# A fused routed-attention and SoLU kernel on one core: a new written order for all engines, and the first one-hot marks copied by three engines

## The chip, the cores and the metric

The kernel runs on one core of a Trainium2 chip. The metric is the device time of one execution in microseconds (us); lower is better. Before the change the median of three runs is 225.78 us (225.64 to 225.80).

The core has a matrix engine (PE, with its weight loads shown apart as PEld), a vector engine (DVE), a scalar engine (ACT), a general engine (POOL) and a queue that issues DMAs (SP). Each works through its own list of instructions in order and waits for the others by semaphores.

## What is computed

Attention with routing: queries and keys of each head are assigned to the nearest of 16 centroids, and a query attends only to keys of its own cluster. The result, read as 3072 tokens of 512 numbers, goes through a feed-forward layer with a SoLU activation and a layer norm.

```python
def _attn_ref(q, k, v, centroids):            # (4, 8, 768, 64), centroids (8, 16, 64)
    ...
    q_assign = np.argmax(np.einsum('bhsd,hcd->bhsc', q_n, c_n), axis=-1)
    k_assign = np.argmax(np.einsum('bhsd,hcd->bhsc', k_n, c_n), axis=-1)
    mask = q_assign[:, :, :, None] == k_assign[:, :, None, :]
    scores = scale * np.matmul(q, k.transpose(0, 1, 3, 2))
    scores = np.where(mask, scores, -1000000000.0)
    ...
    return np.matmul(attn, v)
def _moe_ref(x, w_in, w_out, g_ln):           # (3072, 512), (512, 1024), (1024, 512)
    h = x @ w_in
    ...
    solu = h * sm                             # sm is the softmax of h
    ...
    ln = (solu - mu) / np.sqrt(var + 1e-06) * g_ln
    return ln @ w_out
```

## The kernel before

Work is cut into pairs of heads, four pairs in each of four batches, written `b.p`. For a pair, queries (`i` = 0) and keys (`i` = 1) are loaded, turned so that the head dimension lies on the partitions, and cast to bf16 into a tile `qk`. Beside the 64 numbers of a head, `qk` holds one-hot marks of the token's cluster; the keys' marks and the queries' marks raise the score of matching clusters, so that one matmul gives scores that are already masked, and the exponential with a constant bias does the rest.

All work is described as small named operations. `Weave.add` records each with its engine, its cost in a planner and what it needs; `Weave.queues` puts them on the engines' lists in the order that the text `ORDER` gives: for each engine a row of kinds with repeat counts (`E12` is the next twelve operations of kind `E`). `AWAY` names the operations that run on another engine than their default. The planner's costs do not enter the order of one engine's list, which is read from the text. The kinds that matter here, with the function and line that issues them:

- `ld`, `lv`: loads of queries, keys, values on SP (L366 to 399, L527).
- `tp` (`turn_tokens`, L386, PE): the first batch's tokens turned by matmuls with the identity, into three banks of PSUM in turn; `xa` (`keep_tokens`, L393, ACT or DVE): the copy out of PSUM. The very first pair, `0.0`, is done in two halves, whose number is the last of the name. Later batches are turned by DVE: `xt` (L407).
- `ca` (`cast`, L431 ACT, L433 and L435 DVE or POOL): the cast into `qk`. A half has 64x384 elements, a whole one 64x768. `cv` (L532): the cast of the values. `bl` (L523), `z`, `zo`: memsets.
- `cl` (`clusters`, L450, L445, PE): the products with the centroids. Then a chain on DVE: `tb` turns them back (L459), `mx` takes the largest (L472), `oh` marks it (L484), `ot` turns the marks (L494). `pl` (`place`, L498 to 519) copies the marks into `qk`: four copies for each pair or half (L514; L506 for the other pairs of the first batch), on DVE, POOL, or as a DMA on SP. `place` knows DVE, POOL and SP before.
- `S` (`scores`, L601, PE) for a bank of 512 or 384 scores, `E` (`expo`, L607, ACT), `V` (`values`, L624, PE), `N` (`normalise`, L636 and L649, DVE). There are three score banks and nine tiles of exponentials, used in turn, so `S` waits for the `E` three before it, and `E` for the `V` that has read the tile nine before.
- The feed-forward layer works on blocks of 128 tokens, `f` from 0 to 23: `tx` turns the block (SP; for the last one PE, `ptx`, L688, and a copy on DVE, `tx23`, L691), `h` multiplies with `w_in` (L710, PE), `hm` takes the row maximum (L716, DVE), `ex` the exponential (L722, ACT), `u` the product (L727, DVE), `tu` turns it (SP; for the last two `ptu` on PE, L698, and copies `tu`, L704 DVE or L706 ACT), `bn` and `ag` are row statistics (L738 and L742, DVE), `at` and `al` the factor of the norm (POOL, L748 to 757), `y` multiplies with `w_out` (L771, PE), `sc` scales (L786 ACT or L788 DVE) and `ou` stores. `h` for the second half of block f waits for `u` of block f-1, since the two share a bank.
- `wm` and `fl` (L816) are matmuls on idle data at the start; `lo`, `li`, `wi`, `su`, `me`, `ce`, `gt`, `gk` prepare the weights of the layer.

Resolved into names, the order before begins and ends so:

```
PE    wm tp0.0.0.0 tp0.0.1.0 cp tp0.0.0.1 cl0.0.0 tp0.0.1.1 fl0..fl4 cl0.0.1 fl5..fl8 S0.0 ...
ACT   xa0.0.0.0 xa0.0.1.0 ca0.0.0.0.0 ca0.0.0.1.1 xa0.0.1.1 ca0.0.1.0.1 ca0.0.1.1.0 E0.0 ...
      E0.5 E1.3 E1.4 E1.5 xa0.2.1.0 xa0.2.1.1 E2.0 ...
DVE   cn cb xa0.0.0.1 ca0.0.1.0.0 tb0.0.0 mx0.0.0 oh0.0.0 ot0.0.0 pl0.0.0.1.1 pl0.0.0.0.0 tb0.0.1 ...
POOL  z1 ca0.0.0.0.1 ca0.0.0.1.0 pl0.0.0.1.0 pl0.0.0.0.1 cv0.0.1 z2 bl0.0.0 ...
DVE at the end
      ... hm21 sc17 u21 N38 ag19 ag20 bn21.0 tx23 hm22 bn21.1 sc19 u22 bn22.0 ag21 hm23 bn22.1
      tu22.0 ag22 u23 bn23.0 bn23.1 tu23.1 ag23 sc23.1
```

Of the kernel before, what the change touches and what calls it, by code (L numbers as in the profile page):

```python
# [22 lines left out]
class Weave:  # L23
# [18 lines left out]
    """
    ORDER["PE"] = """
        wm tp2 cp tp cl tp fl5 cl fl4 S3 tp2 S2 tp S cq S tp S2 tp2 S2 V3 S cl S tp2 V3 S gt S tp S
        tp S2 cl S2 V2 S V S2 tp S2 tp S2 V2 S V S2 cl S2 V2 S V2 S3 V S2 V2 S2 V S cl S3 su S2 V3 S
        V S3 V3 S2 V S su S2 V S V3 S3 me S3 V4 S3 cl S3 V4 S2 h S h S2 h S h S2 V3 S2 V h S h V S V
        S h S V S V S h S2 V3 S2 V h S2 h V2 S y3 S2 h3 S3 y V3 h V S2 V2 S cl S3 h2 S2 V3 S y2 S V
        h2 S V y2 S h S V h S2 h S y3 S2 y V3 h S3 cl V2 S V S y S2 y2 S3 V3 S y S2 V3 S2 cl S V S2
        V2 S h S2 V2 S V S h S2 V2 cl V2 S3 y2 S V S2 V y S2 y V2 S3 h2 S V h S h S2 V h S V S V y2
        S h V y2 S2 V S h3 S cl V S2 V2 S h V cl S3 h2 V y V S3 y2 V S h V3 S y S h S2 h2 S3 V2 y h  # L50
        S V S2 y V3 y S3 h3 y S3 V3 S h S V S V cl S V S h S cl V2 S3 y V2 S y S2 y V2 S3 h y V S3 V
        h V2 S3 cl S2 V2 S y3 S2 y S V3 S V S y S2 V S V3 S2 y2 S3 y V2 S2 h V2 S3 h3 S V S2 V y S V
        h2 V2 S y S2 y V y S h2 S3 cl h V S2 V3 S h V2 S3 h2 S y S2 V h S2 V y2 V4 S3 y h S2 h V h V
# [115 lines left out]
def kernel(  # L169
# [11 lines left out]
    nc = tc.nc  # L181
# [4 lines left out]
    NB = 32  # L186
# [1063 lines left out]
```

## Time and profile before

| | |
|---|---|
| median of the runs | 225.78 us |
| the profiled execution: time, span | 225.95 us, 223.9 us |
| busy: PE, DVE, ACT, POOL | 215.1, 197.3, 191.5, 127.1 us |
| granted PE clock | 1.00 throughout |
| first scores begin (L601, PE) | 10.16 us |
| last exponentials of scores begin (L607, ACT) | 200.6 us |
| last store issued | 221.3 us |

The span is the time from the first to the last instruction or transfer of the profiled execution; the rest of its time lies around it. Busy times are sums over one engine, which overlap with those of the others. The chain of waits follows the last instruction back to what released it, step by step.

### The profile page before, as it was taken

How to read it: one execution, taken by the hardware profiler on the slowest of the kernel's cores; microseconds unless marked ns; L12 is line 12 of the kernel's file. 1: busy time of each engine (PE TensorE's matmuls, PEld its weight loads, DVE VectorE, ACT ScalarE, POOL GpSimd, SP SyncE). 2: the span in 40 equal slices, each digit the busy share in tenths (PEclk: the TensorE clock that was granted, in tenths of full speed). 3: DMA queues.
4: the chain of work that ended last, by engine and by line, in shares of the span. 5: the costliest groups of instructions: out<-in, count | busy, mean ns of one | idle time of the engine just before them, and what ended most of it. 6: DMA issues, size and time to landing. Idle time of an engine off the chain costs nothing.

```text
span 223.9 us, 6574 instructions
## 1 busy us (share of the span) xinstructions
PE 215.1 (96%) x2388; PEld 148.1 (66%) x2420; DVE 197.3 (88%) x359; ACT 191.5 (86%) x371; POOL 127.1 (57%) x247
## 2 busy tenths in 40 slices
PE   7899999999999999999999999999999999999993
PEld 3576756677667678776677667777677687754442
DVE  3799899899999989999998989887998889888981
ACT  3689999999998999998889899999999998982362
POOL 3489843964794999547668634943895413031331
PEclk9999999999999999999999999999999999999999
DMA  7998989999898989999999999199931433766622
GB/s 152 353 318 147 249 199 275 290 243 158 132 199 140 232 130 165 193 189 177 183 218 168 184 195 195 65 174 232 236 64 28 79 70 120 96 146 170 176 97 94
DMA packets 125679, 38.80 MB, mean 173 GB/s; under 512 B 115016, under 2 KB 121168, under 8 KB 125648
## 3 DMA queue, kind: packets, MB, share of 16 engines
q1 hardware_dynamic: 123904, 37.87, 80.6%
q10 hardware_dynamic: 1744, 0.52, 1.0%
q8 instruction: 19, 0.31, 0.6%
q14 instruction: 12, 0.10, 0.2%
HBM read 23.11 MB, written 6.29 MB: 131 GB/s over the span
## 4 chain that ended last, share of the span: by engine, by line
PE 86%; ACT 5%; DVE 3%; issue 3%; DMA 1%; POOL 1%; ACTq 0%; DVEq 0%; POOLq 0%
PE sps L601 28%; PE hreg L710 18%; PE yps L771 16%; PE ops L624 14%; ACT e L607 5%; PE csc L450 4%; PE hreg L386 2%; PE hreg L574 1%; PE hreg L771 1%; DMA c_all<-in_centroids_dram 1%; PE csc L445 1%; DVE bs L738 1%; DVE u L727 1%; ACT xt L393 0%; PE hreg L584 0%
## 5 line engine op out<-in xcount | busy, mean ns | idle before, releaser
L607 ACT ACTIVATE e<-sps 128x512 bf16<-128x512 f32 (+1 forms) x294 | 151.0, 599 | 12.2 <-PE sps L601 10.2
L601 PE MATMUL sps<-qk 80*128 80x256 bf16 (+5 forms) x636 | 93.8, 264 | 1.8 <-POOL qk L514 0.7
L601 PEld LDWEIGHTS <-qk 80*128 80x128 bf16 (+1 forms) x636 | 60.2, 121 | 27.9 <-issue 9.0
L624 PEld LDWEIGHTS <-e 128*128 128x128 bf16 x1152 | 50.4, 97 | 12.3 <-issue 1.9
L624 PE MATMUL ops<-v,e 128*128 128x65 bf16 x1152 | 55.0, 193 | 0.1
L710 PE MATMUL hreg<-w_in_sb,xT 128*128 128x512 bf16 x173 | 49.1, 379 | 1.1
L771 PE MATMUL yps<-w_out_c,uT 128*128 128x512 bf16 x171 | 46.4, 379 | 0.6
L727 DVE TENSOR_TENSOR u<-e_sb,hreg 128x1024 bf16<-128x1024 bf16 x24 | 29.0, 1210 | 4.9 <-ACT e_sb L722 4.7
L514 POOL COPY qk<-oht 32x384 f32<-32x384 f32 (+1 forms) x50 | 24.4, 488 | 15.8 <-DVE oht L494 13.6
L738 DVE BATCH_NORM_STATS2 bs<-u 128x6 f32<-128x512 bf16 x48 | 31.5, 676 | 0.2
L716 DVE TENSOR_REDUCE nmax<-hreg 128x1 f32<-128x1024 f32 x24 | 29.0, 1209 | 2.6 <-PE hreg L710 2.2
L722 ACT ACTIVATE e_sb<-hreg,nmax 128x1024 bf16<-128x1024 f32 x24 | 26.9, 1120 | 4.5 <-DVE nmax L716 4.4
L433 POOL CAST qk<-xt 64x768 bf16<-64x768 f32 (+1 forms) x31 | 26.1, 842 | 5.5 <-DVE xt L393 3.9
L771 PEld LDWEIGHTS <-uT 128*128 128x128 bf16 x200 | 18.2, 97 | 12.3 <-DVE uT L704 0.7
L754 POOL TENSOR_SCALAR esq<-es,mv 128x1 f32<-128x1 f32 x24 | 8.5, 355 | 29.0 <-DVE mv L742 20.8
L435 POOL TENSOR_SCALAR qk<-xt 64x768 bf16<-64x768 f32 (+1 forms) x28 | 23.0, 820 | 1.7
L710 PEld LDWEIGHTS <-xT 128*128 128x128 bf16 x192 | 16.8, 97 | 9.4 <-issue 0.6
L407 DVE STREAM_TRANSPOSE xt<-raw 128x768 f32<-128x768 f32 x24 | 22.6, 953 | 0.2 <-DMA raw<-in_q_dram 0.2
L748 POOL TENSOR_SCALAR es<-esum 128x1 f32<-128x1 f32 x24 | 5.3, 221 | 27.6 <-ACT e_sb L722 27.1
L649 DVE TENSOR_TENSOR x<-ops,den 128x256 bf16<-128x256 f32 (+1 forms) x39 | 18.9, 486 | 1.3
L757 POOL TENSOR_TENSOR alpha<-esq,halves 128x1 f32<-128x1 f32 x24 | 13.5, 561 | 2.0
L786 ACT ACTIVATE y<-yps,alpha 128x512 f32<-128x512 f32 x13 | 9.0, 692 | 6.4 <-PE yps L771 6.0
(80 smaller groups left out, 170.1 us busy)
## 6 DMA issues: line engine op xcount, KB each, us to landing
vf<-in_v_dram SPq DMA_DIRECT2D x16, 384.0 KB, 4.4
out_dram<-y SPq DMA_DIRECT2D x23, 256.0 KB, 2.7
raw<-in_q_dram SPq DMA_DIRECT2D x50, 96.0 KB, 3.7
raw<-in_k_dram SPq DMA_DIRECT2D x50, 96.0 KB, 3.0
w_g<-in_moe_w_out_dram SPq DMA_DIRECT2D x4, 512.0 KB, 5.3
w_st<-in_moe_w_in_dram SPq DMA_DIRECT2D x4, 512.0 KB, 5.9
raw<-in_q_dram SPq DMA_DIRECT2D x3, 384.0 KB, 6.3
raw<-in_k_dram SPq DMA_DIRECT2D x3, 384.0 KB, 6.8
```

The costliest lines, as they stand in the source:

```text
L433: VEC[e].tensor_copy(dst, src)
L435: VEC[e].tensor_scalar(dst, src, scalar1=inv_C, scalar2=1.0, op0=Alu.mult, op1=Alu.mult)
L514: ins = VEC[e].tensor_copy(dst.bitcast(F32), src.bitcast(F32).unsqueeze(1) .to_broadcast([NB, 2, n // 2]))
L601: nc.tensor.matmul(sps_[n, k][:, c0:c0 + w], side(b, h // 2, 1, h % 2, keys)[r], side(b, h // 2, 0, h % 2, slice(s0 * P, s0 * P + w))[r])
L607: nc.scalar.activation(es[n, k][:, :w], sps_[n, k][:, :w], Act.Exp, scale=exp_scale, bias=-exp_scale)
L624: nc.tensor.matmul(opss[g][:, s, :VW], es[n, k][:, c0:c0 + P], v1[slot(b, h // 2)][:, h % 2, kt, :VW], start=(kt == 0), stop=(kt == n_t - 1))
L710: uses(nc.tensor.matmul(hreg[:, at(f, f2)[1], :], xTs[f][:, dc, :], w_in_sb[:, dc, f2 * FF2:(f2 + 1) * FF2], start=(dc == 0), stop=(dc == ...
L716: uses(nc.vector.tensor_reduce(ff[f, "nmax"][:], pair_of(f), axis=AXY, op=Alu.max, negate=True), *both(f))
L722: uses(nc.scalar.activation(ff[f, "e"][:], pair_of(f), Act.Exp, bias=ff[f, "nmax"][:], accum_out=ff[f, "esum"][:]), *both(f))
L727: uses(nc.vector.tensor_tensor(ff[f, "u"][:], ff[f, "e"][:], pair_of(f), op=Alu.mult), *both(f))
L738: nc.vector.bn_stats(ff[f, "bs"][:, f2, :], ff[f, "u"][:, f2, :])
L771: ins = nc.tensor.matmul(dst, ff[f, "uT"][:, at(f, f2)[0] * (n_fc // 2) + c, :], w_out_c[:, fc, cols], start=(fc == 0), stop=(fc == n_fc - 1))
```

## The change

The change writes a new `ORDER` for all five engines and a new `AWAY`, gives `place` a branch for ACT, and alters three of the planner's costs (which, as said, don't enter the lists).

```diff
     ORDER["PE"] = """
-        wm tp2 cp tp cl tp fl5 cl fl4 S3 tp2 S2 tp S cq S tp S2 tp2 S2 V3 S cl S tp2 V3 S gt S tp S
+        wm tp2 cp tp cl tp fl5 cl fl3 S3 tp2 S2 cq S tp S tp S2 tp S tp S V3 S cl tp2 V3 S gt S2 tp
...
     ORDER["DVE"] = """
-        cn cb xa ca tb mx oh ot pl2 tb mx oh ot xa3 bl cf cv xa zo xa2 tb ca mx oh gk N ot tb pl mx
+        cn cb ca2 tb mx oh ot pl2 tb mx oh ot xa2 ca xa cf xa2 ca tb mx xa gk oh ot N tb xa mx oh
...
-        hm sc u N ag2 bn tx hm bn sc u bn ag hm bn tu ag u bn2 tu ag sc
+        bn2 hm ag bn ag sc u N bn2 tx hm sc u bn2 hm ag tu ag tu u bn2 tu ag sc2
     ORDER["ACT"] = """
-        wa xa2 ca2 xa ca2 E12 xa2 E6 xa E58 ex E12 ex E8 ex E8 ex E3 sc E5 ca E2 ex E25 ex E9 sc E6
+        wa xa ca xa3 ca pl ca E9 xa E3 ca xa E6 xa E58 ex E13 ex E7 ex E10 ex sc E5 sc E6 ex E9 sc
...
     AWAY.update(dict.fromkeys("""
-        ca0.0.0.0.0 ca0.0.0.1.1 ca1.3.1.1 sc23.0 tu22.1 xa0.0.1.0 xa0.2.1.0 xa0.2.1.1 xa0.3.0.0
+        ca0.0.0.0.0 ca0.2.0.0 ca2.2.1.0 ca2.2.1.1 ca3.0.1.1 pl0.0.0.0.1 sc23.0 xa0.0.0.1 xa0.0.1.0
+        xa0.2.0.1 xa0.2.1.0 xa0.3.0.0
     """.split(), "ACT"))
...
         elif e == "SP":
             ins = nc.sync.dma_start(out=dst, in_=src.unsqueeze(1).to_broadcast([NB, 2, n]))
+        elif e == "ACT":
+            ins = nc.scalar.copy(dst, src.unsqueeze(1).to_broadcast([NB, 2, n]))
...
-    add("wm", "PE", 3.55, -1000, lambda e: [idle(FF2) for _ in range(6)])
+    add("wm", "PE", 3.9, -1000, lambda e: [idle(FF2) for _ in range(6)])
...
-                add(f"tp{t}.{hf}", "PE", 0.7 - 0.2 * hf if halves_of(b, p) else 0.36, first - 15 + i + hf,
+                add(f"tp{t}.{hf}", "PE", (0.5 if i * hf else 0.7) if halves_of(b, p) else 0.36, first - 15 + i + hf,
...
-                costs = ({"DVE": 0.3, "POOL": 0.41} if half else
+                costs = ({"DVE": 0.3, "POOL": 0.41, "ACT": 0.42} if half else
```

The number of `fl` in the text sets how many are made: nine before, eight after. Sixty-three operations change their engine. ACT takes `xa0.0.0.1`, `xa0.2.0.1`, one mark copy (`pl0.0.0.0.1`), the casts `ca0.2.0.0`, `ca2.2.1.0`, `ca2.2.1.1`, `ca3.0.1.1` and the scalings `sc2`, `sc3`, `sc6`, `sc8`, `sc10`, `sc13`, and gives away `xa0.2.1.1`, `ca0.0.0.1.1`, `ca1.3.1.1`, `sc11`, `sc12`, `sc14`, `sc22` and `tu22.1`. POOL's list goes from 212 to 205 operations. Seven mark copies are DMAs on SP, `pl1.0.1.0` and `pl1.0.1.1` the first, in place of four.

The lists begin and end so after the change:

```
PE    wm tp0.0.0.0 tp0.0.1.0 cp tp0.0.0.1 cl0.0.0 tp0.0.1.1 fl0..fl4 cl0.0.1 fl5..fl7 S0.0 ...
ACT   xa0.0.0.0 ca0.0.0.0.0 xa0.0.1.0 xa0.0.0.1 xa0.0.1.1 ca0.0.1.0.1 pl0.0.0.0.1 ca0.0.1.1.0 E0.0 ...
      E0.5 xa0.2.0.1 E1.3 E1.4 E1.5 ca0.2.0.0 xa0.2.1.0 E2.0 ...
DVE   cn cb ca0.0.0.1.0 ca0.0.1.0.0 tb0.0.0 mx0.0.0 oh0.0.0 ot0.0.0 pl0.0.0.1.0 pl0.0.0.1.1 tb0.0.1 ...
POOL  zo ca0.0.0.0.1 cv0.0.0 ca0.0.0.1.1 pl0.0.0.0.0 z1 bl0.0.0 ...
DVE at the end
      ... hm21 ag19 bn20.1 ag20 sc17 u21 N38 bn21.0 bn21.1 tx23 hm22 sc19 u22 bn22.0 bn22.1 hm23 ag21
      tu22.0 ag22 tu22.1 u23 bn23.0 bn23.1 tu23.1 ag23 sc22 sc23.1
```

80 lines of the change are left out of this document (40 added, 40 removed).

## The prediction

> **What bounds the kernel now.** I read the page first (busy shares, chain of waits), then the busy time of each engine by stage, then the timeline of the first 24 us and of the last 18.
>
> ```profile
> PE 215.1 (96%) x2388; PEld 148.1 (66%) x2420; DVE 197.3 (88%) x359; ACT 191.5 (86%) x371; POOL 127.1 (57%) x247
> ...
> PE 86%; ACT 5%; DVE 3%; issue 3%; DMA 1%; POOL 1%; ACTq 0%; DVEq 0%; POOLq 0%
> ```
>
> PE is busy 96% of the span and carries 86% of the chain that ended last. The change takes no PE work away but one filler matmul (`fl8`, about 0.07 us, inside a wait). So the time can change in three places alone: the start, where PE waits; the stretches where another engine fills up and PE waits for it; and the end, where PE's work is no longer the chain.
>
> ```profile
> core 0: us, PE busy (x) PEld busy (x) DVE busy (x) ACT busy (x) POOL busy (x), PEclk, DMA share, GB/s
> ...
> 18.00:22.00 4.00, 3.87 (x43) 2.20 (x41) 3.68 (x10) 4.00 (x11) 3.79 (x6) 1.00 0.72 94
> ...
> 26.00:30.00 4.00, 3.89 (x66) 2.93 (x64) 3.34 (x7) 4.00 (x9) 3.46 (x6) 1.00 0.72 141
> ...
> 45.00:50.00 5.00, 4.94 (x69) 3.82 (x68) 4.82 (x9) 5.00 (x11) 3.31 (x6) 1.00 1.24 261
> 50.00:60.00 10.00, 9.56 (x115) 7.38 (x115) 9.48 (x18) 9.95 (x20) 5.10 (x11) 1.00 0.83 138
> ```
>
> Read the fourth busy column: up to 60 us ACT is as full as PE. In these four rows (23 us) ACT is busy 22.95 and PE 22.26, so PE loses 0.74 us, 3.2%. In the seven rows of 20 us from 60 to 200 PE is busy 138.51 of 140 (1.1% lost) and ACT 130.05 (93%).
>
> **The start.**
>
> ```profile
> 6.85 0.56 DVE L393 COPY xt<-hreg 128x384 f32<-128x384 f32 x1 [0.66 <-PE hreg L386]
> ...
> 7.59 0.37 DVE L459 STREAM_TRANSPOSE cst<-csc 128x192 f32<-128x192 f32 x1
> ...
> 8.83 0.38 DVE L494 STREAM_TRANSPOSE oht<-oh 128x192 bf16<-128x192 bf16 x1
> 9.25 0.58 DVE L514 COPY qk<-oht 32x192 f32<-32x192 f32 x2
> ...
> 9.35 0.76 POOL L514 COPY qk<-oht 32x192 f32<-32x192 f32 x2 [0.77 <-DVE oht L494]
> ...
> 10.16 0.65 PE L601 MATMUL sps<-qk 80*128 80x384 bf16 x3 [0.73 <-POOL qk L514]
> ```
>
> The first cluster products end at 7.27 (their row: 6.74 and 0.53), yet DVE turns them back at 7.59: it is busy with `xa0.0.0.1` and a cast. After the change `xa0.0.0.1` is on ACT and both casts of DVE use data that are ready by 6.5, so the turn waits for PE alone. The later products that end at 15.80 are taken up at 15.90, so I count 0.10 and get 7.37: 0.22 earlier. The chain behind it is unchanged (7.59 to 9.21), and `ot0.0.0` ends at 8.99. Does the new ACT order delay the products? `ca0.0.0.0.0` (0.52) now stands ahead of `xa0.0.1.0`, which ends near 6.45 in place of 6.16; PE is at its transposes until 6.74, so nothing. Past that, 0.3 us of cover is left.
>
> The four mark copies: before two on DVE and two on POOL, to 10.11. After: two on DVE (9.03 to 9.60), one on POOL, one on ACT. POOL has two half casts (0.53 each) and `cv0.0.0` (0.50) ahead, from 7.40 to 9.05, and its mark takes 0.36, to about 9.5. A mark copy on ACT is in no trace; the ACT copy of 384 elements takes 0.48 and the 64x384 cast 0.52, the shortest ACT row (one element) 0.19; I take 0.50, which also ends at 9.6. With a cast (0.52) behind it the exponentials can start at 10.1. So the first scores go from 10.16 to about 9.70: **-0.45** (bounds 0 and -0.55).
>
> The Trainium skill (SBUF — State Buffer, Who interferes with whom) says that GpSimd and a VectorE copy in a two-port mode exclude each other for a whole instruction. By that rule the POOL mark would come behind both DVE marks, near 9.95, and the first scores near 10.05, a gain of 0.1. The rows above disagree: POOL's first copy ran from 9.35 to 9.71 across two DVE copies and took 0.36, against 0.34 for the same copy at 11.89 beside a DVE copy out of PSUM.
>
> **ACT up to 60 us.** How much of the 0.45 lasts depends on ACT, full from 10.5 on.
>
> ```profile
> 14.80 1.25 ACT L607 ACTIVATE e<-sps 128x384 bf16<-128x384 f32 x3 [0.72 <-PE ops L624]
> 16.44 0.86 ACT L393 COPY xt<-hreg 128x384 f32<-128x384 f32 x2 [0.39 <-PE hreg L386]
> ```
>
> After the change ACT gets `ca0.2.0.0` (a 64x768 cast, 0.84 by its one ACT row) ahead of `E2.0`. `xa0.2.0.1` moves into the 0.72 gap (0.40 saved behind it), about 0.12 of the second gap is used, the rest waits for `S2.0`, now behind V1. `E2.0`: -0.45 + 0.84 - 0.40 - 0.12 = **-0.13** (bounds -0.45 and +0.4).
>
> From 22 to 45 us ACT has six gaps behind late PE (0.16, 0.16, 0.18, 0.38, 0.14, 0.16: 1.18). PE is late there mostly behind DVE and POOL: `cl0.3` waits 0.42 for `xa0.3.1.1`, `V6.0` 0.41 for N2, `V10.0` 0.62 for N4, and `S4.0` 0.61 for the POOL mark that ends at 22.10 (PE's spacing from start to start over the usual one of such a group). After the change DVE has 12.3 us of work between N0 and N4 in place of 15.4 (its own durations added up along the written orders), and POOL reaches both marks that `S4.0` needs about 0.9 earlier. All gaps gone would be -1.18, none 0; PE's own work fills most of that time, so I take a third: **-0.4**.
>
> **ACT from 60 to 200 us.** In come three 64x768 casts (0.84) and six scalings (0.69), out go one cast and three scalings: five instructions net, 2 x 0.84 + 3 x 0.69 = 3.75 us. Cover: ACT's 9.95 us of idle time; if all of it were in the way, +3.75. I take it that each fills its neighbourhood of some 4 us, 20 us in all, in which PE then loses 3.2% in place of 1.1%, as in the rows above: **+0.4** (bounds 0 and +3.75). POOL loses 8.6 us of work; it is not the bound. Three more mark DMAs stand in SP's queue net, about 0.6 us of issue each; the loads behind `pl1.0.1.x` land 3.8 us ahead of their use (`ld1.2.0` at 53.06, used at 56.9), so nothing.
>
> **The end.**
>
> ```profile
> 207.47 0.64 DVE L738 BATCH_NORM_STATS2 bs<-u 128x6 f32<-128x512 bf16 x1
> ...
> 208.03 0.41 DVE L691 COPY xT<-xtp 128x512 bf16<-128x512 bf16 x1
> ...
> 208.39 1.22 DVE L716 TENSOR_REDUCE nmax<-hreg 128x1 f32<-128x1024 f32 x1
> ...
> 209.65 1.11 ACT L722 ACTIVATE e_sb<-hreg,nmax 128x1024 bf16<-128x1024 f32 x1 [1.52 <-DVE nmax L716]
> ...
> 210.89 1.22 DVE L727 TENSOR_TENSOR u<-e_sb,hreg 128x1024 bf16<-128x1024 bf16 x1
> ...
> 212.16 0.64 PEld L710 LDWEIGHTS <-xT 128*128 128x128 bf16 x4 [0.22 <-DVE u L727]
> ...
> 213.34 1.22 DVE L716 TENSOR_REDUCE nmax<-hreg 128x1 f32<-128x1024 f32 x1 [0.39 <-PE hreg L710]
> ```
>
> From 207 on this is a closed chain: hm22, ex22, u22, the products of token block 23 (PE waits for u22), hm23, ex23, u23, turn, output. Before, `bn21.1` stands behind hm22; after, ahead of `tx23` and hm22. It starts 0.65 before the next DVE instruction can, so hm22 comes 0.65 later. Earlier, DVE has 1.2 us less ahead of hm21, but `bn20.1`, `ag19`, `ag20` and `sc17` now lie between hm21 and u21 (1.7 us, as long as ex21 and its hops), so u21 gains 0.1. Then `bn22.1` (0.68) also stands ahead of hm23, where 0.39 was idle and `ag21` (0.15) leaves: +0.1. Between hm23 and u23 `tu22.1` (0.41) joins `ag21`, `tu22.0`, `ag22`: 1.2 us, covered by ex23 (1.27 from hm23's end to u23). `sc22` (0.73) on DVE lies in the 1.97 wait ahead of `sc23.1`. Sum 0.65 - 0.1 + 0.1 = **+0.65** (bounds 0, if DVE comes early, and +0.9).
>
> **Sum.** -0.13 - 0.4 + 0.4 + 0.65 = +0.52 on the profiled execution's 225.95 (span 223.9, 2.05 around it, taken as fixed): 226.47. That execution lies 0.17 above the median of the runs, so I forecast 226.3.
>
> **Rivals.**
> - Front gain kept. DVE's lead removes all 1.18 of gaps, ACT's added work finds idle time, and DVE reaches u21 0.6 earlier so that `bn21.1` ends before `h22.1.1`. For it: 15.4 against 12.3 us of DVE work; against it: u21 waits for ex21. -0.13 - 1.18 + 0.1 = -1.2: 224.6; half of it 225.2. It decides from the point where hm22 starts right behind `h22.1.1`.
> - ACT becomes the bound between 102 and 150 us, where its work rises by 2.8 us along the order. Half of 3.75 on the path in place of 0.4: 227.8. Against it: ACT has 7% idle.
> - POOL and DVE exclude each other at the first marks: POOL's mark starts when the second DVE mark ends, the first scores come 0.35 later than summed: 226.65. The 0.36 of POOL's copy speaks against it. (It is the Trainium skill's rule above.)
> - The change doesn't do what it says: PE's order up to `cl0.0.0` is the same in both orders, the products already stand ahead of the last turning of the second half; if ACT's copy is slow as well, nothing is left but reshuffling: 225.8.
>
> **Chances.** Forecast 0.42 (own range 225.9 to 226.8), gain kept 0.33, ACT bound 0.15, exclusion 0.05, no effect 0.05. About 0.2% (0.45 us) is what a measurement tells from no change. Slower by more: 0.28 of the forecast, 0.15, 0.04, together 0.47. Within: 0.14 + 0.06 + 0.01 + 0.05 = 0.26. Faster: 0.27, all of it from the gain kept. The range 224.9 to 227.4 takes in half of each bound.
>
> **What would show it.** First scores at 9.6 to 9.8; `E2.0` 0 to 0.3 earlier than 17.18; ACT gaps from 22 to 45 us near 0.8 in sum; ACT near 133.8 us busy from 60 to 200 and PE below 138.2; at the end two row-statistics instructions ahead of the copy of `xT`, and hm22 beginning 0.5 or more after its last product. I am wrong if hm22 starts right behind its products, or if PE loses less than before from 22 to 200 us.

## The result, and the profile after

The changed kernel takes 228.47 us (median of 4 runs, 228.34 to 229.0), the kernel before beside it 225.79 (225.64 to 226.15): ratio 1.0122, 95% interval 1.0105 to 1.014. Slower was forecast, but by 0.5 us; it is 2.7. The profiled execution took 228.44, its span is 226.7 (before 223.9).

From the page of the changed kernel, the busy shares and the chain that ended last:

```profile
PE 218.5 (96%) x2419; PEld 148.5 (66%) x2419; DVE 200.6 (88%) x358; ACT 193.8 (85%) x376; POOL 122.6 (54%) x240
...
PE 71%; DVE 11%; DMA 10%; issue 2%; SPq 2%; ACT 1%; POOL 1%; DVEq 0%; ACTq 0%
```

PE is busy 96% as before, but it carries only 71% of the chain in place of 86%. ACT's share of the chain fell from 5% to 1%; DVE went from 3% to 11% and transfers from 1% to 10%. So the chain now runs through waits for loads and for DVE, not through ACT.

Busy time by stage of the changed kernel (engines in the order of the first row, then the granted clock, the share of the DMA engines and GB/s):

```profile
core 0: us, PE busy (x) PEld busy (x) DVE busy (x) ACT busy (x) POOL busy (x), PEclk, DMA share, GB/s
20.00:40.00 20.00, 19.28 (x264) 12.25 (x261) 19.42 (x36) 18.97 (x40) 16.61 (x28) 1.00 0.99 255
40.00:60.00 20.00, 19.81 (x246) 14.45 (x244) 17.96 (x33) 19.66 (x40) 10.62 (x18) 1.00 0.88 182
60.00:80.00 20.00, 19.64 (x212) 13.25 (x211) 19.57 (x32) 17.41 (x33) 13.31 (x26) 1.00 1.10 189
80.00:100.00 20.00, 19.93 (x243) 14.63 (x240) 18.99 (x35) 19.38 (x40) 10.46 (x21) 1.00 1.02 167
```

The column to read is the one before the last: the DMA share is 0.88 to 1.10 in these rows. In the same rows of before it is 0.89, 1.02, 1.02 and 0.95, so that the transfers are full is not new. What is new is when they are issued and when they land, as the second loss below shows.

**Where the time went.** Every PE instruction of a trace can be matched with its name in the program. I give each product its mean spacing in the trace of before (scores 0.24 us, values 0.25, first layer 0.34, second layer 0.375, a cluster product 0.78) and ask how much later than before the same sum of work is reached. This lag is good to about 0.1 us; where an order swaps light and heavy products it has bumps of 0.2 to 0.3. Changed kernel minus before, in us, at times of the trace of before:

| at (us of before) | 13 | 25 | 56 | 68 | 97 | 134 | 175 | 212 |
|---|---|---|---|---|---|---|---|---|
| lag | 0.32 | 0.35 | 0.36 | 0.90 | 1.29 | 1.73 | 2.19 | 2.21 |

So 0.36 is lost up to 56 us, 0.54 between 56 and 68, 0.39 up to 97, 0.92 from there to the end of PE's work. The last 0.5 lies behind the last product (from its start to the end of the span: 4.02 in place of 3.53).

The first loss, in the timeline of the changed kernel:

```profile
5.21 0.87 PE L387 MATMUL hreg<-ident_f,raw 128*128 128x128 f32 x3 [0.63 <-DMA raw<-in_k_dram]
...
6.86 0.87 PE L451 MATMUL csc<-xt,c_bd 128*32 128x192 f32 x8
...
8.92 0.51 POOL L535 CAST v<-vf 128x384 bf16<-128x384 f32 x1 [0.91 <-DMA vf<-in_v_dram]
9.00 0.38 DVE L495 STREAM_TRANSPOSE oht<-oh 128x192 bf16<-128x192 bf16 x1
...
9.41 0.73 DVE L517 COPY qk<-oht 32x192 f32<-32x192 f32 x2
9.49 0.54 POOL L434 CAST qk<-xt 64x384 bf16<-64x384 f32 x1
9.66 0.51 ACT L515 COPY qk<-oht 32x384 bf16<-32x384 bf16 x1
...
10.09 0.34 POOL L517 COPY qk<-oht 32x192 f32<-32x192 f32 x1
...
10.48 0.65 PE L604 MATMUL sps<-qk 80*128 80x384 bf16 x3 [0.27 <-POOL qk L517]
```

The first scores start at 10.48: later than before (10.16), not earlier, and 0.78 behind the forecast's 9.70. Two things make that up. The larger comes first: PE waits 0.63 us for the first keys (landed at 5.07, before at 4.64), and the first eight cluster products take 0.87 us in place of the 0.53 that the forecast took from the trace of before. So the marks are turned (`ot0.0.0`) by 9.38 in place of 8.99, and the two copies on DVE, which take 0.73 in place of 0.58, end at 10.14, the one on ACT at 10.17. The smaller is POOL: it stands 0.91 us at `cv0.0.0`, because the first values landed at 8.87 (in the trace of before at 7.76), then casts the key part, and its mark ends at 10.43, 0.26 behind the others.

How early the scores start differs from one execution to the next. In the twelve profiled executions whose lists begin as in the changed kernel they start at 9.48 to 10.82; with the old start (before, e1, e3) at 9.88 to 10.16.

The second loss, in the timeline between 57 and 62 us:

```profile
57.28 0.97 DVE L408 STREAM_TRANSPOSE xt<-raw 128x768 f32<-128x768 f32 x1
...
58.20 1.21 ACT L725 ACTIVATE e_sb<-hreg,nmax 128x1024 bf16<-128x1024 f32 x1
...
59.18 0.98 DVE L408 STREAM_TRANSPOSE xt<-raw 128x768 f32<-128x768 f32 x1 [0.93 <-DMA raw<-in_k_dram]
...
60.09 1.18 DVE L730 TENSOR_TENSOR u<-e_sb,hreg 128x1024 bf16<-128x1024 bf16 x1
...
61.33 0.82 PE L713 MATMUL hreg<-w_in_sb,xT 128*128 128x512 bf16 x3 [0.36 <-DVE u L730]
```

And before, where both turnings run in one piece and PE does not wait:

```profile
56.87 1.83 DVE L407 STREAM_TRANSPOSE xt<-raw 128x768 f32<-128x768 f32 x2
...
58.62 1.18 DVE L727 TENSOR_TENSOR u<-e_sb,hreg 128x1024 bf16<-128x1024 bf16 x1
...
60.13 1.24 PE L710 MATMUL hreg<-w_in_sb,xT 128*128 128x512 bf16 x5
```

In the changed kernel the second turning (`xt1.2.1`) waits 0.93 us for its load `ld1.2.1`, and `u1`, whose input `ex1` is there at 59.49, stands behind it on DVE. From the start of the product ahead of `h2.1.0` (60.59) to `h2.1.0` itself (61.33) PE needs 0.74 us in place of 0.22. `ld1.2.1` was issued at 55.20 and landed at 58.99 (before 54.13 and 56.55): issued 1.07 later, it landed 2.44 later.

### The profile page after: what moved, and what is told of

Read it like the earlier page. It is cut to its first block, busy times and chain, and to the rows that moved or that the text cites. A ratio compares the mean times of both kernels' runs of the same rounds, so it can differ in the third digit from the quotient of the medians.

```text
span 226.7 us, 6602 instructions
## 1 busy us (share of the span) xinstructions
PE 218.5 (96%) x2419; PEld 148.5 (66%) x2419; DVE 200.6 (88%) x358; ACT 193.8 (85%) x376; POOL 122.6 (54%) x240
## 4 chain that ended last, share of the span: by engine, by line
PE 71%; DVE 11%; DMA 10%; issue 2%; SPq 2%; ACT 1%; POOL 1%; DVEq 0%; ACTq 0%
PE sps L604 21%; PE hreg L713 16%; PE yps L774 15%; PE ops L627 12%; PE csc L451 3%; DMA uT<-u 3%; DMA vf<-in_v_dram 2%; DVE u L730 2%; DMA w_st<-in_moe_w_in_dram 2%; DVE xt L408 2%; DMA raw<-in_k_dram 2%; PE hreg L387 2%; DVE bs L741 1%; SPq L400 1%; DMA raw<-in_q_dram 1%
## 5 line engine op out<-in xcount | busy, mean ns | idle before, releaser
L604 PE MATMUL sps<-qk 80*128 80x256 bf16 (+5 forms) x636 | 97.0, 264 | 0.6 <-POOL qk L517 0.3
L713 PE MATMUL hreg<-w_in_sb,xT 128*128 128x512 bf16 x192 | 53.1, 379 | 0.5 <-DVE u L730 0.4
L774 PE MATMUL yps<-w_out_c,uT 128*128 128x512 bf16 x184 | 48.7, 379 | 0.1
L517 POOL COPY qk<-oht 32x384 f32<-32x384 f32 (+1 forms) x46 | 23.1, 502 | 8.9 <-DVE oht L495 4.7
L436 POOL TENSOR_SCALAR qk<-xt 64x768 bf16<-64x768 f32 (+1 forms) x26 | 22.2, 852 | 2.1 <-DVE xt L394 0.2
L434 POOL CAST qk<-xt 64x768 bf16<-64x768 f32 (+1 forms) x25 | 20.5, 818 | 4.7 <-ACT xt L394 3.6
L789 ACT ACTIVATE y<-yps,alpha 128x512 f32<-128x512 f32 x15 | 10.4, 691 | 6.1 <-PE yps L774 5.6
```

Source lines behind the costliest of these rows:

```text
L436: VEC[e].tensor_scalar(dst, src, scalar1=inv_C, scalar2=1.0, op0=Alu.mult, op1=Alu.mult)
L517: ins = VEC[e].tensor_copy(dst.bitcast(F32), src.bitcast(F32).unsqueeze(1) .to_broadcast([NB, 2, n // 2]))
L604: nc.tensor.matmul(sps_[n, k][:, c0:c0 + w], side(b, h // 2, 1, h % 2, keys)[r], side(b, h // 2, 0, h % 2, slice(s0 * P, s0 * P + w))[r])
L713: uses(nc.tensor.matmul(hreg[:, at(f, f2)[1], :], xTs[f][:, dc, :], w_in_sb[:, dc, f2 * FF2:(f2 + 1) * FF2], start=(dc == 0), stop=(dc == ...
L774: ins = nc.tensor.matmul(dst, ff[f, "uT"][:, at(f, f2)[0] * (n_fc // 2) + c, :], w_out_c[:, fc, cols], start=(fc == 0), stop=(fc == n_fc - 1))
```

## The experiments

Each kernel has the lists of the changed kernel, or of the kernel before, written out by name, with the moves shown. Lags are PE's, as above; increments are differences of that lag.

**1. Which stretch of the order costs.** Four hybrids of the two lists, cut by the begin times in the trace of before.

```diff
 e1_front_of_before:  changed lists, begun before 16 us: as before
 e2_front_of_after:   lists of before, begun before 16 us: as changed
 e3_before_to_100:    lists of before to 100 us, changed lists behind
 e4_after_to_100:     changed lists to 100 us, lists of before behind
```

> The changed kernel, but with the old lists and engines for all operations that began before 16 us in the profile of before; the new lists behind that. If the start is to blame (values awaited ahead of a mark copy), this gives back the 0.3 us that the first scores lost and little more: 228.1. If the waits in the body cost the most (theory: transfers that land late behind SP's new order, near 60 and 94 us, and VectorE near 27 and 108 us), nearly all of the loss stays: 227.9 to 228.3. If the casts on ScalarE at the start decide, 227.5 or less.

> The kernel before, but with the new lists and engines for all operations that began before 16 us in the profile of before. Theory: first scores 0.3 us later than before, the rest as before: 226.1. Rival (the new start is neutral and the wait for the first values is chance of one execution): 225.7 or less, and the first values land near 7.8 us.

> Old lists up to 100 us, new lists behind. Theory (most of the loss is made by named waits before 110 us): a quarter to a third of the loss, 226.4 to 226.9. Rival (ScalarE's added work from 100 to 200 us is the bound): two thirds or more of the loss, 227.6 to 228.3.

> New lists up to 100 us, old lists behind. Theory: two thirds of the loss or more, 227.2 to 227.8, with the waits near 60 us (ld1.2.1, u1) and 94 us (tu4, y4) still in the trace. Rival (ScalarE from 100 to 200 us): 226.3 or less.

| run | median us | ratio (95%) | lag at 25 | 56 | 68 | 97 | 212 |
|---|---|---|---|---|---|---|---|
| e1 | 229.16 | 1.0123 (1.0056 to 1.019) | -0.05 | -0.12 | 0.90 | 1.58 | 2.31 |
| e2 | 226.40 | 1.0003 (0.9981 to 1.0025) | -0.60 | 0.25 | 0.25 | 0.25 | 0.38 |
| e3 | 227.01 | 1.0022 (0.999 to 1.0055) | -0.07 | 0.10 | 0.10 | 0.10 | 0.67 |
| e4 | 229.68 | 1.0144 (1.01 to 1.0188) | 0.38 | 0.26 | 1.97 | 2.11 | 3.77 |

None of the four times fell into the range that its theory gave: e1 229.16 (227.9 to 228.3), e2 226.40 (226.1, and its first scores came early, at 9.61, not late), e3 227.01 (226.4 to 226.9), e4 229.68 (227.2 to 227.8). What the four do show is in the lags. With the old start (e1) the loss at the start is gone and the lag at 68 us is the same as in the changed kernel, 0.90: `ld1.2.1` landed at the same time (58.98), and the wait for it takes up whatever start there was. The part behind 100 us costs 0.57 by itself (e3; its time alone does not tell it from before, since the interval holds 1), and the new start alone loses nothing that can be measured (e2), though it gains 0.6 up to 25 us and has lost it by 44. (e4 has 1.5 us at its seam, which belongs to neither order.)

**2. Mend one named wait.** Four single edits on the changed kernel.

```diff
 f1_marks_pool   SP:   tx0 -pl1.0.1.0 -pl1.0.1.1 ld1.2.0.0    POOL: wi2 +pl1.0.1.0 +pl1.0.1.1 pl1.0.0.0
 f2_xt121        DVE:  xt1.2.0 -xt1.2.1 u1 +xt1.2.1 bn1.0
 f3_tu4          SP:   +tu4 ld2.2.0 ld2.2.1.0 ld2.2.1.1 ld2.2.1.2 ld2.2.1 -tu4
 f4_xt231        DVE:  xt2.3.0 +xt2.3.1 -ca2.1.1.1 hm7 +ca2.1.1.1 -xt2.3.1
```

> The changed kernel with one thing undone: the two mark copies pl1.0.1.0 and pl1.0.1.1 go from SP's queue back to POOL. Theory (SP's queue between 40 and 60 us is too full, so ld1.2.1 lands at 58.99, xt1.2.1 and behind it u1 on DVE are late and h2.1.0 waits 0.69 us): the two DMAs are 1.5 us of SP's time at 42.5 to 44.0, so ld1.2.0.0 is issued near 42.5 and ld1.2.1 0.7 to 1.5 us earlier; the wait of h2.1.0 falls from 0.69 to under 0.2 us and the time to about 228.0. Rival (SP paces itself by landings further down the queue, so the room is taken up by other transfers; or what the wait gives is taken again by the next wait): ld1.2.1 lands within 0.3 us of 58.99, or the wait goes and the time stays at 228.3 to 228.6.

> The changed kernel with one VectorE instruction moved: xt1.2.1, which waits 0.9 us for ld1.2.1, stands behind u1 instead of ahead of it. Theory (DVE stands still behind a late transfer, and the products of cluster 2 behind DVE): u1 starts near 58.3 instead of 60.09, the 0.69 us wait of h2.1.0 at 60.5 us goes, PE is 0.5 to 0.7 us earlier from 62 us on and stays so, time 227.8 to 228.0. Rival (ScalarE or VectorE as a whole bound the stretch from 60 to 110 us; the single waits only show where): PE is earlier at 62 us and has lost it again by 110 us; time 228.3 to 228.6.

> The changed kernel with one DMA moved in SP's queue: tu4 (the turned u of cluster 4) stands ahead of ld2.2.0 as it nearly did before the change, five loads earlier. Theory (y4.0 waits for it 0.40 us at 93.3 us): tu4 is issued near 84.4 instead of 87.63 and lands near 88 to 91, the wait of y4.0 goes, time about 228.1; no other wait comes, since the loads behind it are used 3 us and more later. Rival (absorbed): PE earlier at 94 us, nothing left by 110 us, where xt2.3.1 is next, time 228.3 to 228.6.

> The changed kernel with two VectorE instructions moved: xt2.3.1 directly behind xt2.3.0 (ahead of hm7, as before the change), ca2.1.1.1 behind hm7. Theory (VectorE's order makes cl2.3 late by 0.55 us at 109.6): xt2.3.1 ends near 108.0 instead of 109.78, cl2.3 waits under 0.2 us, hm7 is 0.3 us later at most; PE 0.3 to 0.5 us earlier from 111 us on, time 228.0 to 228.2. Rival (ScalarE's load behind 100 us bounds): PE is back at the changed kernel's lag of 1.9 to 2.1 us by 150 us; time 228.3 to 228.6.

| run | median us | ratio (95%) | 56 to 68 us | 68 to 97 | 97 to 212 |
|---|---|---|---|---|---|
| changed | 228.47 | 1.0122 (1.0105 to 1.014) | 0.54 | 0.39 | 0.92 |
| f1 | 227.66 | 1.0076 (1.0029 to 1.0123) | 0.24 | 0.14 | 0.77 |
| f2 | 227.91 | 1.0095 (1.0064 to 1.0126) | 0.67 | 0.15 | 0.77 |
| f3 | 228.04 | 1.0096 (1.007 to 1.0123) | 0.15 | 0.14 | 0.78 |
| f4 | 228.71 | 1.0124 (1.0087 to 1.0162) | 0.95 | 0.15 | 0.79 |

The expectations failed in part. In f1 `ld1.2.1` is still issued at 55.05 and lands at 59.28: it stands behind `tu0`, which waits for `u0`, so two DMAs fewer ahead of it move nothing. In f2 `u1` comes 0.99 earlier (0.46 of it by an earlier start), and `V25.0` waits for `N11` instead: 0.84 us from the start of the product ahead of it in place of 0.43. In f4 the wait of `cl2.3` is gone (0.28 us from the product ahead in place of 0.53), but it is also gone in f1, f2 and f3, which do not touch it, so behind 97 us f4 is like the other three. f3's `tu4` lands at 88.41 in place of 93.79 and the wait of `y4.0` is gone, yet it is gone as well in f1, f2 and f4, where `tu4` landed at 91.4 to 93.1, and all four have the same 0.14 to 0.15. What differs between these runs from 56 to 68 us (0.15 to 0.95) isn't explained by the edit: f3 and f4 change nothing there.

**3. The end, the wait for u1, all of them.**

```diff
 g1_tail   DVE:  bn21.0 -bn21.1 tx23 hm22 +bn21.1
 g2_u1     SP:   -tu0 ld1.2.1 +tu0      DVE: -xt1.2.1 u1 bn1.0 N11 +xt1.2.1
 g3_all    g1, g2, f3 and f4 together;  POOL: -cv0.0.0 (...) pl0.0.0.0.0 +cv0.0.0
```

> The changed kernel with one VectorE instruction moved: bn21.1 stands behind hm22 again instead of ahead of tx23. Theory (the end is a closed chain of VectorE and ScalarE, and bn21.1 is 0.65 us in it; the loss ahead of the end is made before 100 us and stays): tx23 and hm22 start 0.65 us earlier beside ex21 (in the changed kernel ex21 ends 1.55 us later than before the change, hm22 2.25 later; here both about 1.6), all behind them too, time near 227.8. Rival (PE's products are the chain there: its last first-layer product of token block 22 ends 2.21 later than before): hm22 waits for that product, time 228.3 to 228.5.

> The changed kernel with two moves: tu0 (which waits for u0) behind ld1.2.1 in SP's queue instead of ahead of it, and xt1.2.1 on VectorE behind u1, bn1.0 and N11. Theory (u1 is late because VectorE stands at xt1.2.1 for a late load; that wait makes the loss up to 100 us, and the late start is hidden by it): ld1.2.1 is issued near 53.8 and lands near 57 to 58, u1 ends near 59.5 to 60.0 instead of 61.27, h2.1.0 and V25.0 wait under 0.2 us each, PE 0.9 us earlier at 70 us and ex21 0.9 or more earlier; time 227.3 to 227.6. Rival (the next late piece, tu4 behind y4.0 or xt2.3.1 behind cl2.3, takes the gain): earlier at 70 us, under 0.4 us of it left at ex21, time 228.0 to 228.4.

> The changed kernel with all waits named so far mended: the two moves for u1, tu4 ahead of ld2.2.0, xt2.3.1 behind xt2.3.0, bn21.1 behind hm22, and on POOL the cast cv0.0.0 of the late values behind the first mark copy. ScalarE's added casts and scalings stay. Theory (waits behind single transfers and VectorE instructions make all of the loss; ScalarE's 3.75 us more work cost nothing): the sum of the parts, -0.9, -0.3, -0.3 and -0.65, gives 226.0 to 226.5; first scores near 9.7. Rival (ScalarE's load or the general crowding of the transfers between 20 and 140 us holds the rest): ex21 still 1 us or more later than before the change, time 227.0 or more.

g1: 228.0 us, ratio 1.0085 (1.0037 to 1.0134); lag at 212 us 2.15, in the changed kernel 2.21. g2: 228.2, 1.0082 (1.0049 to 1.0115), 1.67. g3: 228.14, 1.009 (1.0047 to 1.0132), 1.65. The end first. The changed kernel:

```profile
209.13 1.28 DVE L741 BATCH_NORM_STATS2 bs<-u 128x6 f32<-128x512 bf16 x2
...
209.97 0.59 PE L713 MATMUL hreg<-w_in_sb,xT 128*128 128x512 bf16 x2
...
210.33 0.41 DVE L694 COPY xT<-xtp 128x512 bf16<-128x512 bf16 x1
...
210.65 1.21 DVE L719 TENSOR_REDUCE nmax<-hreg 128x1 f32<-128x1024 f32 x1
```

and g1, in which only one row statistics instruction stands there:

```profile
209.07 0.68 DVE L804 BATCH_NORM_STATS2 bs<-u 128x6 f32<-128x512 bf16 x1
...
209.91 0.59 PE L776 MATMUL hreg<-w_in_sb,xT 128*128 128x512 bf16 x2
...
210.11 0.42 DVE L757 COPY xT<-xtp 128x512 bf16<-128x512 bf16 x1 [0.35 <-PE xtp L754]
...
210.54 1.23 DVE L782 TENSOR_REDUCE nmax<-hreg 128x1 f32<-128x1024 f32 x1
```

hm22 (the maximum over `hreg`) starts right behind its last product both times: 209.97 + 0.59 = 210.56 against 210.65, and 210.50 against 210.54. With `bn21.1` out of the way DVE stands idle 0.35 and waits for PE. PE is 2.2 us late by then, so the 0.65 is covered: the rival was right. g3 mends the start (exponentials from 9.73 on, the values landing at 8.59) and keeps that up to 56 us (lag -0.08), but 0.81 is lost again up to 68 us: `u1` is on time, but `y0.0` waits about 0.3 us for `tu0`, which the mend put behind `ld1.2.1`, and the turning, now behind `N11`, holds up `hm2`, so that `ex2` waits 0.61 on ACT and the score products there wait for ACT. In g2, which has the same two moves, 0.8 is lost there for the same reason. The mended waits together gave 0.56 us at PE's end (2.21 to 1.65), and 0.44 of that is the start.

**4. ScalarE's added work.**

```diff
 h1_casts       ACT: -ca2.2.1.0 -ca2.2.1.1 -ca3.0.1.1
                POOL: ca2.3.0.0 +ca2.2.1.0 / ca2.3.1.0 +ca2.2.1.1 / bl3.1 +ca3.0.1.1
 h2_all_casts   the same on g3_all
```

> The changed kernel with the three casts that the change moved to ScalarE (ca2.2.1.0, ca2.2.1.1, ca3.0.1.1, 0.84 us each) back on POOL; all waits stay. Theory A (ScalarE's work is the bound from 100 us on, each of its us costs time): its busy time falls by 2.5 us, the last product comes 0.6 to 1.2 us earlier, time 227.2 to 227.8. Theory B (single waits make the loss, ScalarE has idle time for its work): within 0.2 us, 228.3 to 228.6.

> The kernel with all named waits mended, and the three casts back on POOL as well. Theory A: with the waits gone ScalarE's work is what is left, so the casts count more than in the run above; 0.8 to 1.5 us below the kernel with the mended waits alone (227.85 in its profiled execution), 226.3 to 227.0. Theory B (the rest lies in how PE's products were re-ordered, with less of its other work left to fill its waits for the exponentials): within 0.3 us of 227.85.

h1: 228.59 us (226.88 to 229.84), ratio 1.0086 (1.005 to 1.0122); h2: 227.5 (227.34 to 229.58), 1.0079 (1.004 to 1.0117). From 97 to 212 us PE loses 0.52 and 0.54 in them; in ten executions with the casts on ACT (the changed kernel, e1, f1 to f4, g1 to g3, k1) it loses 0.64 to 0.92, mean 0.76. Two later kernels, k2 and m1 of experiment 5, also have the casts on POOL, and m1 has a loss of its own up to 112 us. So the stretch from 112 to 212 us compares best: the ten lose 0.6 to 0.7 there, the four with the casts on POOL 0.3 to 0.4. The three casts, 2.5 us of work, thus cost about 0.25. Of the 0.5 that is left behind 97 us, the lists of before also show 0.12 to 0.15 with the new start (e2, g4, h3); about 0.4 belongs to the rest of the new order. Theory B was right (within 0.2 us in h1, 0.3 in h2) and theory A fell (0.6 to 1.2 in h1): ScalarE's work counts for a tenth of its length. The profile of h1 shows something else besides:

```profile
61.14 0.98 DVE L470 STREAM_TRANSPOSE xt<-raw 128x768 f32<-128x768 f32 x1 [2.39 <-DMA raw<-in_k_dram]
62.04 1.18 DVE L792 TENSOR_TENSOR u<-e_sb,hreg 128x1024 bf16<-128x1024 bf16 x1
```

Nothing of h1 differs from the changed kernel ahead of 100 us, and yet the same wait is 2.39 us in place of 0.93 and costs 2.0 us of lag. The wait for `ld1.2.1` isn't a fixed length; it differs from execution to execution.

**5. The transfers made early.** In the changed order the values `lv1.2` are issued at 48.0 (before: 44.7), `ld1.2.0` behind them 2.8 us later than before, and `ld1.2.1` still 1.07 later. Apart from the two added mark DMAs SP's order there is that of before, so f1 was the undoing; k1 goes further and puts `lv1.2` and `tu0` behind the loads, which then land earlier than in before. k2 adds other mends, m1 one more.

```diff
 k1_transfers         f1, and  SP:  lv1.1 -lv1.2 tx2 ld1.2.0 ... -tu0 ld1.2.1 +tu0 +lv1.2 ld1.3.0.0
 k2_transfers_casts   k1, f3, h1 and cv0.0.0 behind pl0.0.0.0.0
 m1_ex5               k2, and  ACT: -ex5 E42.0 +ex5 E42.1
```

> The changed kernel with its transfers of 40 to 60 us made early: the two mark copies pl1.0.1.x back on POOL, the values lv1.2 (384 KB, wanted at 64 us) behind tu0, and tu0 behind ld1.2.1. Theory (late transfers make u1 late, by an amount that differs between executions): ld1.2.1 lands by 56, u1 ends 6.5 to 7.0 us after u0 as before the change (it was 7.96), h2.1.0 doesn't wait, time 227.3 to 227.8 and less spread between executions. Rival (the order of PE's products and ScalarE's work hold PE there anyway): PE's lag at 68 us is still 0.7 or more above its lag at 55 us, time 228.0 to 228.4.

> The same early transfers, with tu4 ahead of ld2.2.0, the three casts back on POOL and cv0.0.0 behind the first mark copy. By the parts measured so far (start -0.4 where the values land late, u1's wait -0.3 to -0.5, tu4 -0.3, casts -0.3): 226.7 to 227.2; what is left above the kernel before (about 1 us) then belongs to PE's new order. If it comes at 226.3 or less, the parts explain all; at 227.5 or more, one of them is absorbed.

> The kernel with early transfers, tu4 early, the late values behind the first mark copy and the three casts on POOL, and now ex5 behind E42.0 on ScalarE (before the change it stood there; the change puts it ahead). Theory (ex5 ahead of E42.0 waits for hm5 and holds E42, so S43.0 and S43.1 wait): in the profile PE's lag grows by under 0.2 us from 91 to 97 us in place of 0.67, and the last product comes 0.6 to 0.8 us later than before the change in place of 1.24, if the start is alike; about 226.7 in the profiled execution. Rival (a floor set by the order of PE's products): the lag grows by 0.5 or more somewhere between 91 and 110 us all the same; 227.2 or more.

| run | median us | ratio (95%) | 56 to 68 us | 68 to 97 | 97 to 212 | lag at 212 |
|---|---|---|---|---|---|---|
| k1 | 227.67 | 1.0056 (1.0022 to 1.009) | 0.02 | 0.38 | 0.64 | 1.52 |
| k2 | 227.80 | 1.0067 (1.0035 to 1.0098) | 0.02 | 0.79 | 0.53 | 1.21 |
| m1 | 228.23 | 1.0101 (1.0062 to 1.0141) | 0.02 | 1.11 | 0.97 | 1.64 |

The timeline of k1 (DVE and PE):

```profile
57.40 1.83 DVE L471 STREAM_TRANSPOSE xt<-raw 128x768 f32<-128x768 f32 x2
...
59.64 1.22 DVE L793 TENSOR_TENSOR u<-e_sb,hreg 128x1024 bf16<-128x1024 bf16 x1 [0.41 <-ACT e_sb L788]
...
60.92 1.04 PE L776 MATMUL hreg<-w_in_sb,xT 128*128 128x512 bf16 x4
```

Both turnings run back to back, `ld1.2.1` has landed at 54.51 (before 56.55), `u1` waits only for its own input, and PE doesn't wait. In all three executions with early transfers PE loses 0.02 us from 56 to 68 us; in the twelve with the changed order there it loses 0.15 to 2.0. That shows that the late load makes the loss of this stretch: with the load early it is gone in three kernels of three, one execution each. In the times it shows less. The intervals of k1 and k2 (up to 1.009 and 1.0098) end below that of the changed kernel (from 1.0105), but m1's (1.0062 to 1.0141) overlaps it, and k1's median is that of f1 (227.67 and 227.66), where the load stayed late. The rest isn't the sum of parts: in k2 `S43.0` and `S43.1` wait for ACT at 93 us, where `ex5` had waited for `hm5`; with `ex5` behind `E42.0` (m1) PE loses 0.3 more there, waiting for `E42.1`, now behind `ex5`. The theory of m1 fell. What holds PE at 91 to 97 us once it comes early, and the 0.5 behind 97 us, stay open. Two candidates remain: the order of PE's products, and DVE's (in k2 `hm5` begins 0.85 us behind its last product, before 0.07, because DVE is busy). Neither was tried alone.

**6. What the new start is worth.**

```diff
 g4_lo3         e2, and  SP:   ld1.1.0.1 lo2 +lo3 ld1.1.0.2 ld1.1.0 ld1.1.1.0 -lo3
 h3_new_start   g4, and  POOL: -cv0.0.0 (...) pl0.0.0.0.0 +cv0.0.0
```

> The kernel before with the change's order up to 16 us (as in the run with only the new start), and in SP's queue the weight loads lo2 and lo3 moved ahead of ld1.1.0.2. Theory (the transfers between 20 and 140 us are at their limit, so the start's gain was eaten by the one that became late: the product su1 waited for lo3, which landed at 37.1, 0.7 us after it was wanted): lo3 lands near 35.5, su1 and S14.0 don't wait, PE 0.4 to 0.5 us earlier than before the change from 38 us to the end, time 225.4 to 225.7 where the first values land near 7.7. Rival (another transfer or VectorE takes it): again 0.0 to 0.3 us later than before behind 44 us, time 226.0 to 226.4.

> The kernel before with the change's order up to 16 us alone, the weight loads lo2 and lo3 ahead of ld1.1.0.2, and on POOL the cast of the first values behind the first mark copy. Theory (the start of the change is worth 0.3 to 0.45 us when the late values don't hold it and no transfer behind it is late; everything the change loses comes behind 16 us): 225.3 to 225.6, ratio near 0.998. Rival (the start's gain is used up by other late pieces in most executions): 225.8 to 226.0, ratio 0.9995 to 1.0005.

In e2 the gain was lost at one product, `su1`, and in g4 it isn't. First e2, then g4, PE's timeline:

```profile
36.43 1.79 PE L640 MATMUL hreg<-w_g,w_out_c 128*32 128x512 f32 x8
38.15 0.61 PE L667 MATMUL sps<-qk 80*128 80x256 bf16 x4
```

```profile
36.46 1.07 PE L640 MATMUL hreg<-w_g,w_out_c 128*32 128x512 f32 x8
37.46 0.61 PE L667 MATMUL sps<-qk 80*128 80x256 bf16 x4
```

The same eight products took 1.79 us, since the weight load `lo3` landed in their middle (37.1), and 1.07 with `lo3` three places further ahead. g4: 225.82 us, ratio 0.9993 (0.9959 to 1.0028), lag -0.45 at 56 and -0.32 at the end. h3: 225.59, ratio 0.9978 (0.9953 to 1.0002), lag -0.73 at 56 and -0.58 at the end, values landing at 8.29. Of the 0.58 by which its scores start ahead of g4's, 0.30 is a draw: its first cluster products ended that much earlier (6.88 against 7.18). Its start:

```profile
8.69 0.51 ACT L578 COPY qk<-oht 32x384 bf16<-32x384 bf16 x1 [0.27 <-DVE oht L558]
8.69 0.57 DVE L580 COPY qk<-oht 32x192 f32<-32x192 f32 x2
8.80 0.35 POOL L580 COPY qk<-oht 32x192 f32<-32x192 f32 x1 [0.77 <-DVE oht L558]
9.21 0.50 POOL L598 CAST v<-vf 128x384 bf16<-128x384 f32 x1
...
9.34 0.65 PE L667 MATMUL sps<-qk 80*128 80x384 bf16 x3 [0.47 <-DVE qk L580]
```

All marks are there by 9.26 and the late values no longer matter. (Late keys still do: h2 has the cast behind the mark as well, but its first keys landed at 5.34 and its scores start at 10.58.) This is the fastest kernel of the study: faster than the changed one beyond doubt, and than the one before by about 0.2%, with an interval that just reaches 1.

## Why the prediction was wrong, step by step

- **The start (-0.13 at `E2.0`).** It came 0.55 later. The mechanism holds where its premise does: in f2, whose lists begin as the changed kernel's, the values landed at 7.75, the first scores start at 9.48 and `E2.0` comes 0.04 earlier than before; in g3, k2 and m1 (`cv0.0.0` behind POOL's mark) they start at 9.30 to 9.47 and `E2.0` comes 0.19 to 0.37 earlier. The premise failed: the landing times of one execution were taken as fixed. The keys landed 0.43 later than in it, the first cluster products took 0.87 in place of 0.53, and POOL was to do `cv0.0.0` ahead of its mark as if the values were always there at 7.8. In the eighteen profiled executions besides before and e3 they landed between 7.7 and 8.9, in fifteen of them at 8.2 or later, and where `cv0.0.0` stands ahead of the mark the first exponential follows them by some 2 us. (In e3, with the old start, they landed at 8.77 and the exponentials still began at 10.45: there the cast was on DVE, behind more work.) So +0.36 up to 56 us is in part a draw.
- **First marks and the exclusion rule.** The prediction took the rule of the Trainium skill (SBUF — State Buffer, Who interferes with whom), by which a GpSimd instruction and a VectorE copy in a two-port mode block each other for the whole of the one that issued first, to mean that POOL's mark waits for both DVE marks. That did not come: in h3 it starts 0.11 behind the first of them, takes 0.35 and ends before the second does. But the prediction was wrong to say that the rows disagree with the rule, though their records overlap. The second DVE mark of h3 ends at 9.26, 0.11 behind POOL's mark (9.15); in the changed kernel it ends at 10.14, 0.11 behind POOL's cast (10.03). In the twenty traces 40 marks of 32x192 ran on DVE. The 15 that took 0.25 to 0.26 us did not have to wait; the other 25 took 0.29 to 0.60, and every one ends 0.11 or 0.12 us behind the end of a POOL instruction that ran beside it. So a DVE mark that had to wait finishes only once the POOL instruction beside it is done. The traces agree with the rule that the two exclude each other. POOL's casts ahead of a mark thus cost DVE time that the sum had at nothing: 0.73 for the two copies in place of the forecast's 0.57.
- **ACT up to 60 us (-0.4).** Nothing was gained: the lag is 0.40 at 19 us and 0.54 at 44. ACT's gaps behind late PE from 22 to 45 us did fall, to 0.72 in sum (before 1.18), near the 0.8 that was named, but its exponentials run no earlier for it. The term rests on 12.3 us of work of DVE between N0 and N4, with the durations of before taken as fixed; in the changed trace that work takes 14.6. Most of the difference is in the mark copies, `pl0.2.1.1` above all. Here it is in the changed kernel:

```profile
25.55 0.82 POOL L434 CAST qk<-xt 64x768 bf16<-64x768 f32 x1
25.63 1.40 DVE L507 COPY qk<-w_out_c 16x384 f32<-16x384 f32 x1
...
26.32 1.07 POOL L535 CAST v<-vf 128x384 bf16<-128x384 f32 x2
```

and before:

```profile
25.96 1.64 POOL L506 COPY qk<-w_out_c 16x384 f32<-16x384 f32 x3 [0.47 <-DVE w_out_c L491]
...
26.32 0.35 DVE L506 COPY qk<-w_out_c 16x384 f32<-16x384 f32 x1
```

The new order puts it beside POOL's casts, and it takes 1.40 or 1.41 us in all fifteen executions with the changed order there; in the five others (before, e2, e3, g4, h3) it runs beside POOL's copies and takes 0.35 or 0.36. Behind it N2 ends at 28.57, and PE needs 0.74 us from the product ahead to `V6.0` in place of 0.22; at `V12.0`, behind N5, 0.54 in place of 0.22. It is the exclusion of the first marks again: the copy ends at 27.03, 0.21 behind the first of POOL's two value casts (26.82), although that cast began 0.69 after the copy; in before it ends at 26.67, 0.21 behind POOL's copy (26.46). All 38 copies of this shape on DVE that took longer than 0.36 us, of 70 in the twenty traces, end 0.21 or 0.22 us behind the end of a POOL instruction. What this costs in time was not tried by an edit of that alone.

- **SP's queue ("so nothing").** This is the step that failed most. The slack of 3.8 us was that of `ld1.2.0`. The last load of the group, `ld1.2.1`, had 1.2 us (landed 56.55, used 57.76), and it landed 2.44 later; so DVE stood at `xt1.2.1`, `u1` came behind it, and PE lost 0.54 in the profiled execution (0.15 to 2.0 in others), a term that the sum had at nothing. With the load issued early (k1, k2, m1) PE loses 0.02. The shift was taken as the issue time of the added DMAs (0.6 us each), but the queue there is paced by landings: the transfer behind `lv1.2` (`ld1.2.1.2`) is issued 0.2 to 0.4 us behind the landing of `lv1.2` in before, in the changed kernel and in h1. The added DMAs alone are not the cause, though: without them (f1) `ld1.2.1` is issued at 55.05 and lands no earlier. Of the 2.44, 1.07 is the issue, held up behind `tu0`, which waits for `u0` (that ended 0.49 later, at 53.31). The other 1.37 is that the load is under way for 3.79 us in place of 2.42, and why stays open.
- **ACT from 60 to 200 us (+0.4).** Too small, and only part of it has a named cause. PE loses 0.39 from 68 to 97 us, 0.23 of it at `y4.0`, and 0.92 from 97 us on, or 0.76 in the mean of ten executions; the casts are about 0.25 of that, and about 0.4 stays without a cause. ACT's busy time from 60 to 200 us did not rise to 133.8 as said, it is 130.2 (before 130.1): counted up to its 288th exponential, ACT has 3.5 us more of busy time (181.7 against 178.2), but that exponential ends at 198.6 in place of 195.8, so the window holds less of the work. The rival that ACT becomes the bound (227.8) gave the nearest number, and that is luck: its reason is borne out for 0.25 us. POOL was said to lose 8.6 us of work. By the durations of before the sum is 6.3, and its busy time fell by 4.5; nothing follows from it, since POOL isn't the bound.
- **PE below 138.2 as a sign.** "PE loses less than before" was a named sign of being wrong, and PE is busy 139.2 us from 60 to 200 in place of 138.5. It says little: in the trace of before 32 of PE's products have no record (2388 against 2420 weight loads), so its busy time is short. The lag doesn't rest on the records' number, and by it PE loses 1.8 us more than before between 25 and 175 us.
- **The end (+0.65).** It didn't come. The working followed DVE and took PE's products as on time; the text named the sign of being wrong (hm22 right behind its products), and that is what the trace shows. Instead 0.5 us lies behind the last product: the last store's way from issue to landing is 0.3 of it (2.03 in place of 1.74) and the way from there to the end of the span 0.2 (1.09 in place of 0.90). That this 0.5 comes near the +0.65 of the sum is luck.

## What to carry over

The slack of a moved load is that of the last transfer of its group, and a landing time read from one execution is a draw, not a constant: price an order by what happens when the transfer comes a microsecond late. An instruction's duration is no constant either: the same mark copy on DVE took 0.35 us in one order and 1.40 in the other, behind POOL's casts, so work added up from old rows needs a look at what runs beside it in the new order. And records that overlap do not show that two instructions don't exclude each other; compare their ends. A wait on an engine's queue is worth as much as what stands behind it; here a turning that could wait stood ahead of the one instruction that PE needed. Mending waits one by one in a list made for all engines gave little, since the next one was hidden right behind; keeping the old order and taking over only the part that gains (the start) gave a kernel that is no slower. Of the 2.7 us the runs show the cause of the late load (0.54) and of the casts (about 0.25); the start is in part a draw, and the rest stays open.

## What the runs showed of the hardware

- The first values, issued at 3.3 to 3.7 us in every kernel, landed anywhere from 7.7 to 8.9.
- ACT copies a 32x384 mark with a broadcast source in 0.51 us; the 0.50 of the forecast, taken from other ACT rows, held.
- A mark copy on DVE beside a POOL instruction ends a fixed time behind the end of that instruction: 0.11 or 0.12 us for 32x192 (25 copies, 0.29 to 0.60 us long instead of 0.25), 0.21 or 0.22 for 16x384 (38 copies, 0.59 to 1.41 instead of 0.35), in all twenty traces. It works the other way too: the value cast `cv0.2.1` on POOL takes 0.62 or 0.63 us in the fifteen executions in which the long copy ends during it, and 0.50 in the other five.
- The load `ld1.2.1` landed 2.42 us after its issue in before, 3.79 in the changed kernel and 4.23 in f1.
